# A job's float32 products with v issued as one operation, and the clamp of the weights moved from VectorE to GpSimd

## The chip, the cores and the metric

The kernel runs on one core of a Trainium2 chip. The time is that of one execution on the device, in microseconds (us). One core has five engines that work at their own pace and meet at semaphores: TensorE (PE in the profile, its weight loads PEld), VectorE (DVE), ScalarE (ACT), GpSimd (POOL), and SyncE (SP), which here only issues transfers. Each engine takes its instructions strictly in program order.

## The reference

Causal attention with a decay, over 8 batches of 8 heads (576 positions of 64 elements each), and behind it a layer of two matrices with a squared ReLU between them:

```
scores = q @ k.T / sqrt(64) + cum[:, None] - cum[None, :]     # cum = cumsum(log(clip(f)))
scores = where(above the diagonal, -1e9, scores)
attn = exp(scores - max) / (sum + 1e-9)
x = attn @ v                                                   # 4608 tokens x 512
out = maximum(x @ w_in, 0) ** 2 @ w_out                        # 512 -> 2048 -> 512
```

The two weight matrices come as 64-bit floats.

## The kernel before

**A table of operations.** The program is not written in the order in which it runs. It lists some 6,700 small operations, each with what it needs, which buffers it takes and gives back, a priority, and a cost from hand-written formulas (`pe`, `dve`, `act`, `pool`, `dma`). `Order.run` plays them through and emits each operation for the engine on which it can start soonest; this order is then fixed, and every engine runs its part of it one instruction after the other. So a changed cost, need or buffer moves instructions on all engines.

**Attention** is cut into 72 jobs. Jobs 0 to 7 (LOW) hold the first 256 positions of two heads of batches 0 and 1, jobs 8 to 23 (HIGH) the other 320 positions of one such head, the rest (FULL) a whole head. A job has units, one for each tile of 128 keys: 4 in a LOW job, 5 in a HIGH one, 6 in a FULL one. For a job, `mm` and `top` (lines 712 and 720) find each row's maximum on TensorE and VectorE, a small transfer (`col`, line 729) puts the maxima into a row of the operands, and then for each unit there is a score of two products (764, 768), the exponential on ScalarE (774), the mask on the diagonal tile on GpSimd (777), and the product with v, `av`. Jobs 0 to 27 are "whole": their exponentials stay in float32, and `av` is a single matrix product in TensorE's float32 mode (line 849), which takes four passes over the columns. The jobs behind them split the exponentials and v into two parts each and make three fast products of them (852 to 854). The results are copied to `xt` (873), and the sums (879, 882) go through two trips to memory (926, 934, 941) to be inverted and spread, after which `divide` (954) finishes a pair of heads.

**The layer** works on chunks of 256 tokens: 18 chunks, each with 16 steps of a first product (`m1`, line 1045), ReLU and square, and a second product (`m2`, 1074). Chunk 0 needs jobs 0 to 3, chunk 1 jobs 4 to 7; these two run side by side.

**The weights**, 32 tiles of 128 by 512, are turned from 64-bit words to a pair of fast-mode halves while chunk 0 runs: a transfer issued by GpSimd (432), the magnitude on ScalarE (435), then on VectorE the clamp of the exponent (439), `rebias` (443), `top` (450), `bottom` (456), a copy (316), and `lower` (464). Step `f` of chunk 0 cannot start before tiles `2f` and `2f + 1` are done.

**Buffers.** The exponentials of a whole job go in turn to the buffers named `ph` and `pl`, of which there are three each; a buffer is free again when its `av` is done. Two more, named `p`, serve the other jobs.

Of the kernel before, what the change touches and what calls it, by code (L numbers as in the profile page):

```python
# [9 lines left out]
F32 = mybir.dt.float32  # L10
# [4 lines left out]
ALU = mybir.AluOpType  # L15
# [79 lines left out]
class Order:  # L95
# [17 lines left out]
    def add(self, key, ways, emit, after=(), take=(), give=(), prio=0.0, slack=0.0):  # L113
        op = Op()
        op.key, op.ways, op.emit, op.prio, op.slack = key, ways, emit, prio, slack
        op.take, op.give = list(take), list(give)
        for b in op.give:
            b.users += 1
        op.then, op.ready, op.left = [], 0.0, 0
        op.number = len(self.ops)  # L120
        self.ops.append(op)
        assert key not in self.keys, key
        self.keys[key] = op
        op.left = list(after)
# [65 lines left out]
def pe(*columns, four=False):  # L190
    t = sum(1.68 * n + 10 if four else max(n / 2.2 + 3, 55) for n in columns)
    return "PE", t, t + 165, None


def dve(n, sources=1, psum=False):
    if psum:
        return "DVE", 70 + 1.04 * n, 160 + 1.04 * n, None
    per = 0.54 if sources == 1 else 1.045
    return "DVE", 65 + per * n, 150 + per * n, n >= 64
# [10 lines left out]
def pool(n, sources=1):  # L210
    return ("POOL", 200 + 2.1 * n, 250 + 2.1 * n, True) if sources == 2 else ("POOL", 60 + 1.85 * n, 60 + 1.85 * n, None)
# [8 lines left out]
def decay_attention_relu2_kernel(  # L220
# [18 lines left out]
    nc = tc.nc  # L239

    NH, D, _, S = qk.shape
    P = 2 * D
# [3 lines left out]
    NT, DM = out.shape  # L246
# [10 lines left out]
    MAG_LOW, MAG_HIGH = struct.unpack("<2f", struct.pack("<2I", 0x38000000, 0x47EFFFFF))  # L257
# [5 lines left out]
    DUAL = True  # L263
    BE = 2
    NLOW = BE * NPAIR
    DIRECT = 2
    SLACK_G, SLACK_C = 1500, 600

# [19 lines left out]
    add = order.add  # L288
# [5 lines left out]
    def named(name, shape, dtype):  # L294
        return lambda i: wk.tile(shape, dtype, name=f"{name}{i}", bufs=1)
# [4 lines left out]
    def bank(use):  # L300
# [7 lines left out]
            x=2, r=1, g=1, gh=2, gl=2, osb=2,  # L308
# [3 lines left out]
    def buf(kind, make=None):  # L312
        return Buffer(pools[kind], make)
# [102 lines left out]
    def weight(i):  # L416

        temp = buf("osb", named("osb", [P, DM], F32))
# [17 lines left out]

        def clamp(e):

            nc.vector.tensor_scalar(temp.tile, temp.tile, MAG_LOW, MAG_HIGH, ALU.max, ALU.min)

        def rebias(e):
            wi = temp.tile.bitcast(I32)
# [25 lines left out]
        w = lambda x, j=i: ("w", j, x)  # L468
# [6 lines left out]
        elif i >= 24:  # L475
            after += [("score", g, len(jobs[g]["units"]) - 1) for g in range(SETS)]
        p = weight_prio(i)
        add(w("stage"), [dma(8 * P * DM, "POOL", 2)], stage, after, prio=p)
        add(w("mag"), [act(DM)], magnitude, [w("stage")], take=[temp], prio=p)
        add(w("clamp"), [dve(DM)], clamp, [w("mag")], prio=p)  # L480
        add(w("rebias"), [dve(DM)], rebias, [w("clamp")], prio=p)
        add(w("top"), [dve(DM, 2)], top, [w("rebias")], prio=p)
        add(w("bottom"), [dve(DM, 2)], bottom, [w("top")], prio=p)
# [9 lines left out]
    LOW, HIGH, FULL = range(3)  # L493
    jobs = [
        dict(
            kind=LOW, heads=(2 * g, 2 * g + 1),
# [5 lines left out]
            kind=HIGH, heads=(h,),  # L502
# [5 lines left out]
            kind=FULL, heads=(h,),  # L508
# [26 lines left out]
    def job(g):  # L535
        st = jobs[g]
        kind, whole, units = st["kind"], st["whole"], st["units"]
        heads, h = st["heads"], st["heads"][0]
        b = h // H
        p = job_prio(g)  # L540
# [92 lines left out]
        give = [raw]  # L633
# [119 lines left out]
        for u, (i, j, q0, q1) in enumerate(units):  # L753
# [1 line left out]
            n, o = q1 - q0, i * QA  # L755
            ps = bank("s")
            if whole:
                pt = buf(("ph", "pl")[u % 2], named(("ph", "pl")[u % 2], [P, 448], F32))
            else:
                pt = buf("p", named("p", [P, 448], F32))  # L760

# [66 lines left out]
            jobs[g - 1]["den"] if g % 2 else buf("den", named("den", [P, S], F32))  # L828
        )
        done_copies = []  # L830
        for u, low in parts:
            i, j, q0, q1 = units[u]
            kn = KT[j][1]
            group = groups[i, low]
# [18 lines left out]
                nc.tensor.matmul(a[:D, oo], vvl, ph.tile[:, ii], start=False, stop=False)  # L853
                nc.tensor.matmul(a[:D + 1, oo], vvh, ph.tile[:, ii], start=False, stop=final)  # L854

            key = ("av", g, u) if low or kind == HIGH or u < NU - 2 else ("avh", g, u)
            n = s1_ - s0
            take = [acc] if first and (kind != LOW or i == 0) else []
            give = [x for x in (ph, pl) if x]
# [1 line left out]
            need = need + [last_av] + ([("v", g)] if whole else [("vl", g)])  # L861
            if whole and kind != LOW:
                need.append(("ones", g))
            add(key, [pe(n, four=True) if whole else pe(n, n, n)], av, need, take=take, give=give, prio=p - 0.4)
            last_av = key
            if final:
                def copy_x(e, acc=acc, i=i, low=low):
                    m = QA if low else S - QA
# [302 lines left out]
```

## Time and profile before

| | |
|---|---|
| median of 3 runs | 1214.35 us (1210.73 to 1215.1) |
| the profiled execution's own time | 1216.67 us |
| its span, from the first to the last instruction | 1214.9 us |
| TensorE busy | 1168.1 us, 96% of the span |
| VectorE, ScalarE, GpSimd busy | 684.7, 819.1, 392.5 us |
| mean granted clock of TensorE | 0.990 of full speed |

The profile's times are those of one profiled execution. An engine's busy time counts its own instructions; a busy TensorE is not TensorE at its peak, since the ends of its products are modelled and a product that waits inside counts as busy. The granted clock is the share of 2.4 GHz that TensorE was given: 1.00, or 0.50, which is 1.2 GHz.

### The profile page before, as it was taken

What the parts mean: (1) busy time and instruction counts of PE and PEld (TensorE: products, weight loads), DVE (VectorE), ACT (ScalarE), POOL (GpSimd) and SP (SyncE); (2) the same over time, 40 slices, a digit from 0 to 9 for tenths busy, and PEclk for the clock granted to TensorE, in tenths of its full rate; (3) what the DMA queues carried; (4) which work ended last, traced back from release to release, by engine and by line L of the source; (5) the groups of instructions that cost most, each with busy time, mean ns of one, the idle gap of its engine ahead of it and who ended that gap; (6) DMA issues with size and microseconds to landing.
All of it is one profiled execution on the core that took longest, in us unless ns stands there. A gap on an engine that the chain in (4) does not pass through costs nothing.

```text
span 1214.9 us, 23061 instructions
## 1 busy us (share of the span) xinstructions
PE 1168.1 (96%) x7572; PEld 1038.6 (85%) x7572; DVE 684.7 (56%) x1897; ACT 819.1 (67%) x2129; POOL 392.5 (32%) x593
## 2 busy tenths in 40 slices
PE   3779999999999999999999999999999999999998
PEld 2567777788998999999999999999999999999997
DVE  6779888973666656666667664256565642121111
ACT  3578776775876878787787776577767774454443
POOL 4524443412443444444344444034433420000000
PEclk9979999999999999999999999999999999999999
DMA  4455555421211212122212212021221110000000
GB/s 102 126 119 135 127 136 136 109 72 42 58 43 42 60 42 60 42 60 57 60 42 44 58 42 60 18 42 43 59 42 44 42 34 12 18 19 1 19 18 19
DMA packets 118869, 69.86 MB, mean 57 GB/s; under 512 B 98172, under 2 KB 102300, under 8 KB 118748
## 3 DMA queue, kind: packets, MB, share of 16 engines
q10 hardware_dynamic: 49408, 30.42, 10.5%
q1 hardware_dynamic: 63868, 20.12, 7.6%
q0 software_dynamic: 5472, 17.83, 5.1%
q8 instruction: 61, 1.00, 0.4%
q14 instruction: 60, 0.49, 0.1%
HBM read 58.14 MB, written 9.88 MB: 56 GB/s over the span
## 4 chain that ended last, share of the span: by engine, by line
PE 86%; DVE 5%; DMA 4%; issue 2%; ACT 1%; POOL 1%; SPq 0%; ACTq 0%; DVEq 0%; POOLq 0%
PE bank L1045 32%; PE bank L1074 31%; PE bank L764 4%; PE bank L712 4%; PE bank L768 4%; PE bank L849 3%; PE bank L854 3%; PE bank L853 3%; PE bank L852 3%; DMA w<-tcol 1%; DMA den<-rdr 1%; DVE bank L720 1%; DMA rdr<-cmp 1%; DMA up<-tcol 1%; DMA qkraw<-in_qk 1%
## 5 line engine op out<-in xcount | busy, mean ns | idle before, releaser
L1074 PE MATMUL bank<-w,gh 128*128 128x512 f32 x1152 | 411.8, 398 | 0.5 <-DVE w L464 0.4
L1045 PE MATMUL bank<-xh,w 128*128 128x256 f32 x2304 | 325.8, 284 | 2.7 <-ACT r L1051 1.0
L1045 PEld LDWEIGHTS bank<-xh,w 128*128 128x128 f32 x2304 | 303.8, 190 | 13.8 <-ACT r L1051 1.4
L1063 DVE TENSOR_TENSOR gl<-g,gh 128x256 fp32r<-128x256 f32 x288 | 143.6, 498 | 261.2 <-ACT gh L1060 187.0
L1074 PEld LDWEIGHTS bank<-w,gh 128*128 128x128 f32 x1152 | 216.9, 188 | 40.8 <-DVE w L464 1.0
L1074 PE MATMUL bank<-w,gl 128*128 128x512 f32 x576 | 227.3, 395 | 0.4 <-DVE gl L1063 0.4
L1051 ACT ACTIVATE r<-bank 128x256 f32<-128x256 f32 x288 | 110.3, 383 | 141.0 <-PE bank L1045 130.8
L720 DVE CUSTOM_DVE_ANT_0 bank<-bank,mz 128x448 f32<-128x448 f32 (+4 forms) x320 | 137.9, 432 | 113.9 <-PE bank L712 110.5
L777 POOL TENSOR_SCALAR_AFFINE_SELECT p<-p 128x128 f32<-128x128 f32 (+1 forms) x220 | 77.3, 353 | 332.0 <-ACT p L774 329.4
L1045 PE MATMUL bank<-xl,w 128*128 128x256 f32 x1152 | 183.6, 281 | 0.1
L1045 PEld LDWEIGHTS bank<-xl,w 128*128 128x128 f32 x1152 | 157.3, 190 | 0.3 <-DVE xl L1008 0.3
L805 DVE TENSOR_TENSOR pl<-p,ph 128x320 fp32r<-128x320 f32 (+3 forms) x220 | 134.5, 615 | 38.7 <-ACT ph L802 37.4
L1060 ACT ACTIVATE gh<-r 128x256 fp32r<-128x256 f32 x288 | 119.9, 416 | 46.4 <-PE bank L1074 38.3
L621 POOL TENSOR_TENSOR st<-qkraw,up 64x576 fp32r<-64x576 f32 x88 | 132.4, 1504 | 28.2 <-DVE up L316 13.6
L764 PE MATMUL bank<-up 67*128 67x192 f32 (+3 forms) x364 | 122.9, 338 | 5.0 <-DMA up<-tcol 3.0
L712 PE MATMUL bank<-up 66*128 66x448 f32 (+1 forms) x352 | 113.7, 330 | 14.2 <-DMA up<-w 14.0
L802 ACT CAST ph<-p 128x320 fp32r<-128x320 f32 (+3 forms) x220 | 98.0, 447 | 43.4 <-PE bank L854 16.8
L774 ACT ACTIVATE p<-bank 128x320 f32<-128x320 f32 (+4 forms) x264 | 101.5, 389 | 37.4 <-DVE pl L805 17.5
L1074 PEld LDWEIGHTS bank<-w,gl 128*128 128x128 f32 x576 | 108.8, 189 | 14.6 <-DVE gl L1063 1.1
L1055 ACT ACTIVATE g<-r 128x256 f32<-128x256 f32 x259 | 106.1, 410 | 3.4 <-DVE gl L1063 0.7
L768 PE MATMUL bank<-st 128*128 128x192 f32 (+3 forms) x364 | 108.0, 298 | 0.0
L712 PEld LDWEIGHTS bank<-up 66*128 66x128 f32 x352 | 65.5, 189 | 18.7 <-issue 14.3
(103 smaller groups left out, 1635.3 us busy)
## 6 DMA issues: line engine op xcount, KB each, us to landing
qkraw<-in_qk ACTq DMA_DIRECT2D x48, 288.0 KB
v<-in_v ACTq DMA_DIRECT2D x64, 160.0 KB
out<-osb SPq DMA_DIRECT2D x35, 256.0 KB
w<-in_w_in POOLq DMA_DIRECT2D x32, 256.0 KB, 3.7
w<-in_w_out POOLq DMA_DIRECT2D x32, 256.0 KB, 4.6
den<-rdr SPq DMA_DIRECT2D x48, 144.0 KB
up<-tcol SPq DMA_DIRECT2D x232, 0.5 KB
qkraw<-in_qk ACTq DMA_DIRECT2D x11, 224.0 KB
```

Source lines behind the costliest of these rows:

```text
L621: (nc.vector if e == "DVE" else nc.gpsimd).tensor_tensor(out=out, in0=in0, in1=in1.bitcast(F32), op=ALU.subtract,)
L712: nc.tensor.matmul(ps.tile[:m, :n], r2[:D + 2, o + q0:o + q0 + m], kl0[:D + 2, o + k0:o + k0 + n], start=True, stop=True,)
L720: nc.vector.tensor_tensor_reduce(out=ps.tile[:m, :n], in0=ps.tile[:m, :n], in1=mz[:m, mo:mo + n], op0=ALU.add, op1=ALU.min, scale=-1.0, sc ...
L764: nc.tensor.matmul(ps.tile[:kn, :n], kl0[:D + 3, o + k0:o + k0 + kn], r2[:D + 3, o + q0:o + q1], start=True, stop=False,)
L768: nc.tensor.matmul(ps.tile[:kn, :n], l2[:, o + k0:o + k0 + kn], r1[:, o + q0:o + q1], start=False, stop=True,)
L805: nc.vector.tensor_tensor(out=pl.tile[:kn, :n], in0=pt.tile[:kn, :n], in1=ph.tile[:kn, :n].bitcast(F32), op=ALU.subtract,)
L1045: nc.tensor.matmul(ph.tile[:, :T], w[:, s, cc], x[:, cc, :], start=(cc == 0 and k == 0), stop=(cc == NCC - 1 and k == 2),)
L1051: nc.scalar.activation(out=r.tile, in_=ph.tile[:, :T], func=AF.Relu)
L1055: nc.scalar.activation(out=g.tile, in_=r.tile, func=AF.Square)
L1060: nc.scalar.activation(out=gh.tile, in_=r.tile, func=AF.Square)
L1063: nc.vector.tensor_tensor(out=gl.tile, in0=g.tile, in1=gh.tile.bitcast(F32), op=ALU.subtract)
L1074: nc.tensor.matmul(po, x[:, ts], w[:, s], start=(fc == 0 and k == 0), stop=(fc == NF - 1 and k == 2),)
```

## The change

In a whole job the products with v are collected and issued as one operation, back to back: the four of a LOW job, the five of a HIGH job, and in a FULL job the first four and then the last three. Such an operation needs the exponentials and masks of all its units, and gives all their buffers back together. A table `WHERE` says to which kind of buffer each unit's exponential goes; the third unit now goes to one of the two `p`. The clamp of the weights is issued to GpSimd, with the cost `pool(512)` in the table.

```
@@ -263,6 +263,8 @@
     DUAL = True
     BE = 2
     NLOW = BE * NPAIR
+    WHERE = ("ph", "pl", "p", "ph", "pl", "ph", "pl")
+    TOGETHER = [4, 5, 4]
     DIRECT = 2
     SLACK_G, SLACK_C = 1500, 600
 
@@ -436,7 +438,7 @@
 
         def clamp(e):
 
-            nc.vector.tensor_scalar(temp.tile, temp.tile, MAG_LOW, MAG_HIGH, ALU.max, ALU.min)
+            nc.gpsimd.tensor_scalar(temp.tile, temp.tile, MAG_LOW, MAG_HIGH, ALU.max, ALU.min)
 
         def rebias(e):
             wi = temp.tile.bitcast(I32)
@@ -477,7 +479,7 @@
         p = weight_prio(i)
         add(w("stage"), [dma(8 * P * DM, "POOL", 2)], stage, after, prio=p)
         add(w("mag"), [act(DM)], magnitude, [w("stage")], take=[temp], prio=p)
-        add(w("clamp"), [dve(DM)], clamp, [w("mag")], prio=p)
+        add(w("clamp"), [pool(DM)], clamp, [w("mag")], prio=p)
         add(w("rebias"), [dve(DM)], rebias, [w("clamp")], prio=p)
         add(w("top"), [dve(DM, 2)], top, [w("rebias")], prio=p)
         add(w("bottom"), [dve(DM, 2)], bottom, [w("top")], prio=p)
@@ -755,7 +757,8 @@
             n, o = q1 - q0, i * QA
             ps = bank("s")
             if whole:
-                pt = buf(("ph", "pl")[u % 2], named(("ph", "pl")[u % 2], [P, 448], F32))
+                x = WHERE[u]
+                pt = buf(x, named(x, [P, 448], F32))
             else:
                 pt = buf("p", named("p", [P, 448], F32))
 
@@ -828,7 +831,10 @@
             jobs[g - 1]["den"] if g % 2 else buf("den", named("den", [P, S], F32))
         )
         done_copies = []
-        for u, low in parts:
+
+        size = TOGETHER[kind] if whole else 1
+        together = []
+        for x, (u, low) in enumerate(parts):
             i, j, q0, q1 = units[u]
             kn = KT[j][1]
             group = groups[i, low]
@@ -853,7 +859,8 @@
                 nc.tensor.matmul(a[:D, oo], vvl, ph.tile[:, ii], start=False, stop=False)
                 nc.tensor.matmul(a[:D + 1, oo], vvh, ph.tile[:, ii], start=False, stop=final)
 
-            key = ("av", g, u) if low or kind == HIGH or u < NU - 2 else ("avh", g, u)
+            end = parts[min(x - x % size + size, len(parts)) - 1]
+            key = ("av", g, *end)
             n = s1_ - s0
             take = [acc] if first and (kind != LOW or i == 0) else []
             give = [x for x in (ph, pl) if x]
@@ -861,8 +868,23 @@
             need = need + [last_av] + ([("v", g)] if whole else [("vl", g)])
             if whole and kind != LOW:
                 need.append(("ones", g))
-            add(key, [pe(n, four=True) if whole else pe(n, n, n)], av, need, take=take, give=give, prio=p - 0.4)
-            last_av = key
+            if whole:
+                together.append((av, n, need, take, give))
+                if (u, low) == end:
+                    avs, ns, needs, takes, gives = zip(*together)
+                    together = []
+
+                    def all_av(e, avs=avs):
+                        for f in avs:
+                            f(e)
+
+                    add(
+                        key, [pe(*ns, four=True)], all_av, sum(needs, []), take=sum(takes, []), give=sum(gives, []), prio=p - 0.4,
+                    )
+                    last_av = key
+            else:
+                add(key, [pe(n, n, n)], av, need, take=take, give=give, prio=p - 0.4)
+                last_av = key
             if final:
                 def copy_x(e, acc=acc, i=i, low=low):
                     m = QA if low else S - QA
```

Three places of the order show what moved. On TensorE, at the first jobs (L849 before and L855 now are products with v, L764/L767 and L768/L771 the two products of a score, L712/L714 products for the maxima; `bank_244` before and `bank_271` now are the result of job 0), before:

```order
L849 MATMUL bank_244<-ph_228,w_83 65x256
L764 MATMUL bank_248<-up_71 128x128
L768 MATMUL bank_248<-st_77 128x128
L712 MATMUL bank_251<-w_74,w_73 128x256
L849 MATMUL bank_244<-pl_237,w_83 65x128
L712 MATMUL bank_259<-w_74,w_73 128x128
L849 MATMUL bank_244<-ph_246,w_83 65x256
L764 MATMUL bank_271<-up_72 128x256
L768 MATMUL bank_271<-st_78 128x256
```

and now:

```order
L767 MATMUL bank_246<-up_71 128x128
L771 MATMUL bank_246<-st_77 128x128
L714 MATMUL bank_249<-w_74,w_73 128x256
L714 MATMUL bank_256<-w_74,w_73 128x128
L767 MATMUL bank_264<-up_72 128x256
L771 MATMUL bank_264<-st_78 128x256
L714 MATMUL bank_268<-w_74,w_73 128x256
L855 MATMUL bank_271<-ph_228,w_83 65x256
L855 MATMUL bank_271<-pl_237,w_83 65x128
L855 MATMUL bank_271<-p_244,w_83 65x256
L855 MATMUL bank_271<-ph_252,w_83 65x128
```

The four products stand together behind the job's last score and the first scores and maxima of the next jobs, where they used to stand each behind its own mask.

On GpSimd, at the masks of jobs 2 to 4 (L777/L780), before:

```order
L777 AFFINE_SELECT ph_344<-ph_344 128x128
L777 AFFINE_SELECT pl_347<-pl_347 128x128
L777 AFFINE_SELECT ph_373<-ph_373 128x128
L777 AFFINE_SELECT pl_378<-pl_378 128x128
L777 AFFINE_SELECT ph_411<-ph_411 128x128
L777 AFFINE_SELECT pl_427<-pl_427 128x128
L777 AFFINE_SELECT ph_443<-ph_443 128x128
L777 AFFINE_SELECT pl_455<-pl_455 128x128
```

and now, with the first two clamps (L441) and a transfer of a weight tile (L434):

```order
L780 AFFINE_SELECT ph_336<-ph_336 128x128
L780 AFFINE_SELECT pl_352<-pl_352 128x128
L780 AFFINE_SELECT p_381<-p_381 128x128
L780 AFFINE_SELECT ph_384<-ph_384 128x128
L441 TENSOR_SCALAR osb_408<-osb_408 128x512
L780 AFFINE_SELECT ph_436<-ph_436 128x128
L780 AFFINE_SELECT pl_439<-pl_439 128x128
L780 AFFINE_SELECT p_443<-p_443 128x128
L780 AFFINE_SELECT ph_463<-ph_463 128x128
L434 DMA w_479<-in_w_in 128x2x256 x2
L441 TENSOR_SCALAR osb_475<-osb_475 128x512
```

A clamp stands ahead of the four masks of job 3, and another ahead of those of job 4.

On SyncE's queue, at jobs 6 and 7 (`w_73<-tcol` and `w_75<-tcol` are the maxima of jobs 6 and 7, L729/L731, four of each; `den<-rdr` is the spread of the inverted sums of jobs 2 and 3, L941/L963), before:

```order
L729 DMA w_73<-tcol_574 1x128x1 x2
L941 DMA den_420<-rdr_107 64x2x256 x2
L729 DMA w_73<-tcol_574 1x128x1 x2
L729 DMA w_75<-tcol_618 1x128x1 x2
L926 DMA cmp_642<-den_562 128x1x8
L577 DMA up_71<-cum_dr 2x576
L729 DMA w_75<-tcol_618 1x128x1 x2
```

and now:

```order
L731 DMA w_73<-tcol_533 1x128x1 x4
L956 DMA rdr_107<-cmp_526 128x8
L731 DMA w_75<-tcol_601 1x128x1
L579 DMA up_71<-cum_dr 2x576
L731 DMA w_75<-tcol_601 1x128x1 x2
L963 DMA den_429<-rdr_107 64x2x256 x2
L731 DMA w_75<-tcol_601 1x128x1
```

The spread stood between the maxima of job 6 and now stands ahead of the last of job 7.

## Rows read from the trace of the kernel before

**Rows 1.** The page: busy time by engine; the granted clock in 40 slices.
```profile
PE 1168.1 (96%) x7572; PEld 1038.6 (85%) x7572; DVE 684.7 (56%) x1897; ACT 819.1 (67%) x2129; POOL 392.5 (32%) x593
...
PEclk9979999999999999999999999999999999999999
```

**Rows 2.** Stretches in us: length, busy time by engine, granted clock, DMA share, GB/s.
```profile
18.00:74.00 56.00, 38.12 (x142) 30.10 (x143) 35.69 (x110) 28.39 (x72) 22.79 (x46) 0.85 0.47 113
74.00:100.00 26.00, 23.37 (x133) 18.66 (x132) 22.14 (x63) 22.66 (x57) 10.79 (x20) 0.93 0.51 131
100.00:130.00 30.00, 30.00 (x183) 25.28 (x182) 27.80 (x69) 23.32 (x58) 13.07 (x23) 1.00 0.45 119
130.00:270.00 140.00, 133.69 (x769) 106.90 (x769) 116.27 (x297) 98.96 (x247) 52.46 (x96) 0.99 0.49 121
270.00:320.00 50.00, 50.00 (x324) 43.91 (x325) 22.06 (x72) 32.02 (x80) 13.53 (x24) 1.00 0.17 36
320.00:1215.00 895.00, 889.83 (x6018) 810.93 (x6017) 446.65 (x1254) 606.80 (x1607) 272.07 (x365) 1.00 0.17 40
```

**Rows 3.** Waits of PE from 17 to 100 us: total, times, longest.
```profile
PE bank L764 <- DMA w<-tcol: 6.3, 3, 3.8
PE bank L849 <- POOL ph L777: 5.8, 4, 3.2
PE bank L764 <- DMA up<-tcol: 3.0, 2, 1.9
```

**Rows 4.** Timeline of PE at 228 us: start, length, instruction.
```profile
228.61 0.39 PE L1074 MATMUL bank<-w,gl 128*128 128x512 f32 x1
228.85 0.40 PE L1074 MATMUL bank<-w,gh 128*128 128x512 f32 x1
229.17 0.33 PE L849 MATMUL bank<-pl,v 64*65 64x64 f32 x2
...
229.68 0.31 PE L768 MATMUL bank<-st 128*128 128x320 f32 x1
229.84 0.70 PE L849 MATMUL bank<-ph,v 128*65 128x320 f32 x2
...
230.52 0.32 PE L768 MATMUL bank<-st 128*128 128x320 f32 x1
230.67 0.52 PE L1045 MATMUL bank<-xh,w 128*128 128x256 f32 x3
```

**Rows 5.** Line 439, the clamp: ns shortest/median/longest, first and last start.
```profile
L439 DVE TENSOR_SCALAR osb<-osb x32: 408/420/516, 46.3 to 245.0; 128x512 f32<-128x512 f32 x32
```

**Rows 6.** Lines 777 and 621 on POOL, in the same form.
```profile
L777 POOL TENSOR_SCALAR_AFFINE_SELECT pl<-pl x60: 228/312/1334, 19.8 to 306.2; 128x128 f32<-128x128 f32 x40, 64x64 f32<-64x64 f32 x20
L777 POOL TENSOR_SCALAR_AFFINE_SELECT ph<-ph x40: 282/299/2002, 19.6 to 302.2; 128x128 f32<-128x128 f32 x40
...
L621 POOL TENSOR_TENSOR st<-qkraw,up x88: 1410/1430/2016, 290.0 to 972.0; 64x576 fp32r<-64x576 f32 x88
```

**Rows 7.** Groups on POOL, 60 to 150 us: count, busy us, mean ns, idle before.
```profile
L777 POOL TENSOR_SCALAR_AFFINE_SELECT ph<-ph 128x128 f32<-128x128 f32 x12 | 6.8, 569 | 13.4 <-ACT ph L774 13.4
L777 POOL TENSOR_SCALAR_AFFINE_SELECT pl<-pl 128x128 f32<-128x128 f32 x12 | 5.3, 442 | 32.3 <-ACT pl L774 32.3
```

**Rows 8.** Timelines of POOL and of DVE at 90 us.
```profile
90.50 2.00 POOL L777 TENSOR_SCALAR_AFFINE_SELECT ph<-ph 128x128 f32<-128x128 f32 x1
...
90.47 0.68 DVE L450 SCALAR_TENSOR_TENSOR osb<-w,osb 128x512 int32<-128x512 int32 x1
91.07 0.68 DVE L464 TENSOR_TENSOR w<-osb,w 128x512 fp32r<-128x512 f32 x1
91.67 0.68 DVE L456 SCALAR_TENSOR_TENSOR osb<-w,osb 128x512 int32<-128x512 int32 x1
```

**Rows 9.** Timeline of PE at 193 us, with idle time before it; chain of waits there.
```profile
193.37 1.18 PE L849 MATMUL bank<-pl,v 128*65 128x320 f32 x2 [1.35 <-POOL pl L777]
...
186.34 5.26 DMA den<-rdr
```

More of the change, by code (lines that the diff above doesn't have):

```diff
@@ L265, in decay_attention_relu2_kernel @@
     NLOW = BE * NPAIR
+    WHERE = ("ph", "pl", "p", "ph", "pl", "ph", "pl")
+    TOGETHER = [4, 5, 4]
     DIRECT = 2
@@ L437, in clamp @@
         def clamp(e):
-            nc.vector.tensor_scalar(temp.tile, temp.tile, MAG_LOW, MAG_HIGH, ALU.max, ALU.min)
+            nc.gpsimd.tensor_scalar(temp.tile, temp.tile, MAG_LOW, MAG_HIGH, ALU.max, ALU.min)
         def rebias(e):
@@ L479, in weight @@
         add(w("mag"), [act(DM)], magnitude, [w("stage")], take=[temp], prio=p)
-        add(w("clamp"), [dve(DM)], clamp, [w("mag")], prio=p)
+        add(w("clamp"), [pool(DM)], clamp, [w("mag")], prio=p)
         add(w("rebias"), [dve(DM)], rebias, [w("clamp")], prio=p)
@@ L757, in job @@
             if whole:
-                pt = buf(("ph", "pl")[u % 2], named(("ph", "pl")[u % 2], [P, 448], F32))
+                x = WHERE[u]
+                pt = buf(x, named(x, [P, 448], F32))
             else:
@@ L830, in job @@
         done_copies = []
-        for u, low in parts:
+        size = TOGETHER[kind] if whole else 1
+        together = []
+        for x, (u, low) in enumerate(parts):
             i, j, q0, q1 = units[u]
@@ L854, in av @@
                 nc.tensor.matmul(a[:D + 1, oo], vvh, ph.tile[:, ii], start=False, stop=final)
-            key = ("av", g, u) if low or kind == HIGH or u < NU - 2 else ("avh", g, u)
+            end = parts[min(x - x % size + size, len(parts)) - 1]
+            key = ("av", g, *end)
             n = s1_ - s0
@@ L863, in job, with all_av @@
                 need.append(("ones", g))
-            add(key, [pe(n, four=True) if whole else pe(n, n, n)], av, need, take=take, give=give, prio=p - 0.4)
-            last_av = key
+            if whole:
+                together.append((av, n, need, take, give))
+                if (u, low) == end:
+                    avs, ns, needs, takes, gives = zip(*together)
+                    together = []
+                    def all_av(e, avs=avs):
+                        for f in avs:
+                            f(e)
+                    add(
+                        key, [pe(*ns, four=True)], all_av, sum(needs, []), take=sum(takes, []), give=sum(gives, []), prio=p - 0.4,
+                    )
+                    last_av = key
+            else:
+                add(key, [pe(n, n, n)], av, need, take=take, give=give, prio=p - 0.4)
+                last_av = key
             if final:
```

## The prediction

> **What bounds the kernel now.** I read the page first. TensorE is busy 96% of the span, no other engine over 67% [rows 1], so the end moves only where TensorE gets less to do or stands idle less. The table of stretches says where it is idle: 17.9 us of 56 before 74 us, 2.6 of the next 26, nothing from 100 to 130, 6.3 of 140 to 270, nothing to 320, and behind that 5.2 of 895 [rows 2]. All whole jobs and all clamps lie before 320 us, so what the change can give or take has to come out of these 26.8 us of idle time (17.9 + 2.6 + 6.3), or be added to them. VectorE is the fullest of the others just there: 27.8 of 30 us and 116.3 of 140 [rows 2]. The clock matters as well: the row of the page gives 7 tenths in the third slice, and the first stretch has 0.85 on average [rows 1, 2], so TensorE spends part of the LOW jobs at 1.2 GHz. Its waits there are for transfers of the maxima (6.3 and 3.0 us) and for masks from GpSimd (5.8 us) [rows 3].
>
> **The products as one operation.** The number of products, 140 (8 x 4 + 16 x 5 + 4 x 7), and their columns stay. What could be saved is a cost of going from the fast mode to float32 and back. The timeline shows none for products with 128 keys: from the start of one with 320 columns at 229.84 to the next kind of work at 230.67 are 0.83 us, of which the score between them takes two products of about 0.15 (230.52 to 230.67 for one), and the 0.53 left are four passes of 320 columns at 2.4 GHz, 4 x 320 / 2400 = 0.53 [rows 4]. The product with 64 keys does cost more: from 229.17 to 229.84 less the same 0.30 are 0.37 us, where its four passes of 64 columns take 0.11, and the step to it is 0.32 instead of 0.24 [rows 4]. That makes 0.34 us too much in each of the 20 HIGH and FULL whole jobs, 6.8 us in all. In the new order this product still stands between products with 128 keys, so whatever is paid to enter and leave the 64 rows should stay: I take 0, with 6.8 us gained as the other bound.
>
> What the grouping adds is delay. In a LOW job the first three products used to run while later masks were still to come; now all four follow the last mask, three of them later than before. Three quarters of 4 x 768 columns are 2304, 1.9 us at 1.2 GHz. That delays the job's result, and with it chunk 0, only where the results of jobs 2 and 3 end last. They need not: the transfer that held TensorE longest there is that of the maxima, up to 3.8 us [rows 3], which stood behind the spread of the inverted sums in SyncE's queue. In the new queue the spread stands ahead of the last maximum of job 7, and not between those of job 6, so the wait moves one job on and does not go. I take 0 for the LOW jobs, between 5 us lost (the burst of 1.9 us and one further wait like the mean of the masks' and the maxima's longest, 3.2 to 3.8) and 5 us gained (the 6.3 us of waits for maxima all but gone).
>
> **The clamp leaves VectorE.** 32 clamps at a median of 0.42 us, between 46 and 245 us [rows 5], are 13.4 us less for VectorE, 7% of its time there. TensorE stands idle 8.9 us between 74 and 270 us (2.6 + 6.3) [rows 2]. No gain can pass that; below, nothing is gained if none of it hangs on VectorE. Much of it shows as waits for transfers and for ScalarE and GpSimd, with VectorE somewhere ahead of them, so I take a third, 3.0 us.
>
> **The clamp arrives on GpSimd.** The trace has no such operation there. One source and one result over 64 and 128 columns take 0.23 and 0.29 us at best (the mask), so 512 columns at that slope, about 1 ns a column, make 0.29 + 384 x 0.001 = 0.7 us; two sources over 576 columns take 1.43 us [rows 6], and by columns 512 / 576 x 1.43 = 1.27. I take 1.0, between them, as it has one source and four times the columns. But GpSimd is not alone: from 60 to 150 us the masks of 128 columns take 0.50 us on average ((6.8 + 5.3) / 24) [rows 7] instead of 0.29, and one took 2.00 us while VectorE ran three instructions with two tensors each, back to back from 90.47 to 92.35 [rows 8]. So a clamp is 1.0 x 0.50 / 0.29 = 1.7 us in this stretch, and 32 of them 55 us, on an engine that is busy 52.5 of 140 us and 13.1 of 30 [rows 2]. It has the room. The cost is order: behind a clamp in GpSimd's queue stand masks, behind a mask stands the product, and now a whole job's products. Such a wait is seen at 193 us: a division at the head of the queue waited for a transfer (5.26 us on the chain), the mask behind it was late, TensorE stood 1.35 us [rows 9]. The clamp's own head-of-queue wait is for the magnitude on ScalarE; and `rebias` on VectorE now waits for GpSimd, with maxima queued behind it. I charge 1.5 us: one clamp in eight (4) shows as a wait of 0.4. Bounds: nothing, if all masks keep their slack; 11 us, if one in three shows as 1 us.
>
> The Trainium skill (GPSIMD Engine Reference, Key points) says that GpSimd shares its SBUF interfaces with VectorE and contends with VectorE's instructions that use two ports or two SBUF inputs. The mask of 2.00 us agrees; taken alone the rule speaks against this change, and its result is the second rival below.
>
> **The sum.** 0 for the products, 0 for the LOW jobs, -3.0 for VectorE, +1.5 for GpSimd: -1.5 us. The profiled execution took 1216.67 us, 1.8 more than its span and 2.3 more than the median of 1214.35; from the median this gives 1212.8, said as 1213. A measurement of this kernel can tell about 0.5% from no change, 6.1 us: faster is below 1208.3, slower above 1220.4.
>
> **The rivals.**
> *VectorE was the brake after all.* It is over 90% busy from 100 to 130 us and 83% from there to 270 [rows 2]. If all 8.9 us of idle time behind 74 us go, and some 2 to 5 of the LOW jobs' waits, the time is 1214.35 - 11 to - 14, about 1202. For it: the idle time ends where VectorE's load ends, at 270 us. Against: TensorE is never idle from 100 to 130 us, where VectorE is fullest.
> *GpSimd becomes the brake.* Clamps in front of masks, drawn out by VectorE's two-tensor instructions; if one in three costs TensorE 1 us, 11 us come on top of no gain: 1225. It decides from a clamp of about 2.5 us, or when magnitudes come late. For it: the mask of 2.00 us. Against: GpSimd idles over half of this time, and its wait of 5.26 us at 193 us cost TensorE only 1.35.
> *The LOW jobs get later.* The three products behind the last mask and one more wait: +5 to +8 against -1.5, 1219 to 1221. For it: 17.9 us of idle time show that nothing is spare there. Against: at 1.2 GHz TensorE has other maxima and scores to do meanwhile.
> *The two parts do nothing that counts.* 1214, within my forecast's own spread.
>
> **How the numbers follow.** My forecast with the last case, 1208 to 1219: 0.50. First rival 0.27, second 0.15, third 0.08, half of it on either side of the bound. Faster 0.27 and 0.02 from the forecast's edge: 0.29. Slower 0.15 + 0.04: 0.19. Same: 0.52. Below 1203 lies a little over a third of the first rival, 0.10, and above 1223 two thirds of the second, 0.10: the range is 1203 to 1223.
>
> **What would show it.** The 128-key products should still take 0.53 us for 320 columns within a group, and the 64-key one 0.34 too much; if the latter is gone, that step was wrong and up to 6.8 us are gained. VectorE's busy time should fall by about 13 us; GpSimd's clamps should take 1.0 us alone and 1.7 on average. TensorE's idle time from 74 to 270 us should go from 8.9 to about 7, with more of it put down to masks. The first `m1` should start at about the same time. I am wrong if the LOW jobs end several us earlier or later (their clock may change with the bursts), or if the work behind 320 us, which I left alone, takes another time than now.

## The result, and the profile after

The changed kernel took 1218.95 us (median of 11 runs, 1213.09 to 1222.26) where the kernel before took 1215.01 (11 runs, 1210.73 to 1218.66): a ratio of 1.0036, 95% interval 1.002 to 1.0052. It is slower by 0.36%, 3.9 us, where 1.5 us less was forecast.

The page of the changed kernel, busy time by engine, granted clock, and the chain that ended last, by engine:

```profile
PE 1167.0 (96%) x7572; PEld 1033.7 (85%) x7572; DVE 685.5 (56%) x1872; ACT 805.7 (66%) x2122; POOL 447.1 (37%) x625
...
PEclk9689999899999999999999999999999999999999
...
PE 81%; POOL 4%; DVE 4%; DMA 4%; issue 3%; ACT 2%; SPq 0%; ACTq 0%; DVEq 0%; POOLq 0%
```

GpSimd is 54.6 us busier than in [rows 1], which looks like the forecast's 55 us of clamps, but is not: the 32 clamps take 64.9 us, and the masks 9.5 less than before (112.8 against 122.3). VectorE gave up 13.7 us of clamps and is as busy as before over the whole span (685.5 against 684.7). On the chain that ended last GpSimd has 4%.

The same stretches as in [rows 2], of the changed kernel (length, busy time of TensorE, its weight loads, VectorE, ScalarE and GpSimd, granted clock, DMA share, GB/s; the last one ends with its span):

```profile
18.00:74.00 56.00, 38.26 (x162) 29.30 (x163) 35.32 (x112) 34.10 (x84) 31.25 (x54) 0.73 0.47 117
74.00:100.00 26.00, 21.84 (x129) 16.76 (x128) 21.62 (x55) 19.59 (x51) 14.88 (x23) 0.99 0.52 129
100.00:130.00 30.00, 29.37 (x169) 23.39 (x170) 26.73 (x63) 23.02 (x57) 22.74 (x26) 1.00 0.58 141
130.00:270.00 140.00, 130.91 (x750) 105.25 (x749) 112.49 (x267) 89.45 (x232) 86.36 (x108) 0.96 0.41 111
270.00:320.00 50.00, 50.00 (x315) 42.39 (x314) 20.92 (x66) 30.12 (x77) 14.04 (x25) 1.00 0.18 40
320.00:1220.50 900.50, 893.55 (x6045) 813.90 (x6043) 454.28 (x1278) 602.46 (x1613) 269.97 (x370) 1.00 0.16 40
```

TensorE's idle time from 74 to 270 us is 4.16 + 0.63 + 9.09 = 13.9 us instead of 8.9, and its clock from 130 to 270 is 0.96 instead of 0.99. Before 74 us the idle time is the same (17.7 against 17.9), but the first `m1` starts at 72.8 us instead of 74.1. So 1.3 us are won ahead of it and 5.0 lost behind it, 3.7 in all, near the 3.9 between the medians. (The two profiled executions lie 5.6 us apart, 1222.26 and 1216.67.)

The clock of the first stretch, 0.73 here and 0.85 in [rows 2], can't be read off that column: it counts all time ahead of the trace's first record of the clock as 1.00. In the kernel before that record, a rise, comes at 53.6 us. Ahead of it products of 256 columns start 0.21 to 0.22 us after each other, which is 256 / 1200, where from 80 us on they start 0.12 us after each other:

```profile
34.41 0.41 PE L764 MATMUL bank<-w,w 67*128 67x256 f32 x1
34.63 0.41 PE L768 MATMUL bank<-w,w 128*128 128x256 f32 x1
34.84 0.31 PE L712 MATMUL bank<-w,w 66*128 66x128 f32 x1
```

So from 18 to 74 us the kernel before had 2.4 GHz for 3.4 us only (a mean of 0.53), and the changed kernel, whose first record is a rise at 23.5 us, had it for 20.5 us (0.68). The clock of the LOW jobs went up with the change, not down.

Waits of TensorE in the changed kernel, 17 to 100 us (total, times, longest), which answer to [rows 3]:

```profile
PE bank L855 <- POOL ph L780: 6.0, 1, 6.0
PE bank L855 <- POOL pl L780: 3.8, 1, 3.8
PE bank L767 <- issue: 3.5, 1, 3.5
```

and from 100 to 330 us:

```profile
PE bank L1096 <- DVE w L466: 5.8, 6, 2.2
PE bank L714 <- DVE tcol L722: 2.8, 4, 1.3
```

In the LOW jobs the waits for the maxima's transfers have gone from the head of the list, and two long ones for the group's last mask stand there. They belong to the group and not to the clamp: they end at 30.9 and 35.8 us, ahead of the first clamp at 41.6. Behind 100 us no mask is waited for: what TensorE waits for is `lower` of a weight tile (`L466`), the last step of the way on which the clamp stands. The clamp's own row (ns shortest/median/longest, first and last start) and who waited for it:

```profile
L441 POOL TENSOR_SCALAR osb<-osb x32: 1907/1933/2853, 41.6 to 241.5; 128x512 f32<-128x512 f32 x32
...
who waited for it (us, times):
  DVE osb L445: 12.2, 13
```

The shortest of 32 took 1.91 us and the median 1.93. One clamp beside which VectorE ran nothing at all (at 221.8 us) took 1.93. So it is the price of the instruction alone, where the forecast had 1.0. `rebias` on VectorE waited 12.2 us for it. One such place on the chain of waits (start, length, what), and the end of it on TensorE's timeline:

```profile
184.68 2.37 POOL osb L441
...
188.03 0.72 POOL w L434
...
189.27 3.07 DMA den<-rdr
...
192.48 1.18 POOL xt L976
193.66 1.89 POOL osb L441
195.55 0.75 POOL w L434
...
197.46 2.37 POOL osb L441
...
199.85 0.45 DVE osb L445
...
204.12 0.61 DVE w L466
```

```profile
204.78 0.80 PE L1096 MATMUL bank<-w,gh 128*128 128x512 f32 x1 [2.22 <-DVE w L466]
```

From 184 to 200 us the chain runs through GpSimd: three clamps, the transfers of the next weight tiles that it issues (`L434`, 0.72 and 0.75 us), and a division (`L976`) that stood at the head of its queue for a transfer of 3.07 us with a clamp behind it. The tile is late, TensorE stands 2.22 us. Its clock is at 1.2 GHz from 204.4 to 207.8 us and, around the next such place, from 228.3 to 235.2; before, it fell once in this stretch, for 3.4 us.

### The profile page after: what moved, and what is told of

It is laid out like the page before. It is cut to its first block, busy times and chain, and to the rows that moved or that the text cites. A ratio compares the mean times of both kernels' runs of the same rounds, so it can differ in the third digit from the quotient of the medians.

```text
span 1220.5 us, 22937 instructions
## 1 busy us (share of the span) xinstructions
PE 1167.0 (96%) x7572; PEld 1033.7 (85%) x7572; DVE 685.5 (56%) x1872; ACT 805.7 (66%) x2122; POOL 447.1 (37%) x625
## 4 chain that ended last, share of the span: by engine, by line
PE 81%; POOL 4%; DVE 4%; DMA 4%; issue 3%; ACT 2%; SPq 0%; ACTq 0%; DVEq 0%; POOLq 0%
PE bank L1096 31%; PE bank L1067 30%; PE bank L767 3%; PE bank L714 3%; PE bank L771 3%; PE bank L860 3%; PE bank L859 3%; PE bank L858 2%; PE bank L855 2%; DMA den<-rdr 2%; POOL osb L441 2%; DMA rdr<-cmp 1%; POOL w L434 1%; DVE bank L722 1%; DVE st L623 0%
## 5 line engine op out<-in xcount | busy, mean ns | idle before, releaser
L1085 DVE TENSOR_TENSOR gl<-g,gh 128x256 fp32r<-128x256 f32 x288 | 147.4, 512 | 263.7 <-ACT g L1077 220.7
L780 POOL TENSOR_SCALAR_AFFINE_SELECT p<-p 128x128 f32<-128x128 f32 (+1 forms) x248 | 84.4, 342 | 340.9 <-ACT p L777 337.3
L777 ACT ACTIVATE p<-bank 128x320 f32<-128x320 f32 (+4 forms) x292 | 110.8, 383 | 38.8 <-DVE pl L808 15.9
L714 PE MATMUL bank<-up 66*128 66x448 f32 (+1 forms) x352 | 110.1, 321 | 18.4 <-DMA up<-w 10.6
L767 PE MATMUL bank<-up 67*128 67x192 f32 (+3 forms) x364 | 113.1, 312 | 2.1 <-DMA up<-tcol 1.9
L771 PE MATMUL bank<-st 128*128 128x192 f32 (+3 forms) x364 | 107.5, 297 | 0.0
L714 PEld LDWEIGHTS bank<-up 66*128 66x128 f32 x352 | 64.6, 187 | 23.0 <-issue 14.5
```

The costliest lines, as they stand in the source:

```text
L714: nc.tensor.matmul(ps.tile[:m, :n], r2[:D + 2, o + q0:o + q0 + m], kl0[:D + 2, o + k0:o + k0 + n], start=True, stop=True,)
L767: nc.tensor.matmul(ps.tile[:kn, :n], kl0[:D + 3, o + k0:o + k0 + kn], r2[:D + 3, o + q0:o + q1], start=True, stop=False,)
L771: nc.tensor.matmul(ps.tile[:kn, :n], l2[:, o + k0:o + k0 + kn], r1[:, o + q0:o + q1], start=False, stop=True,)
L777: nc.scalar.activation(out=pt.tile[:kn, :n], in_=ps.tile[:kn, :n], func=AF.Exp, scale=SCALE)
L1085: nc.vector.tensor_tensor(out=gl.tile, in0=g.tile, in1=gh.tile.bitcast(F32), op=ALU.subtract)
```

## The experiments

All ratios are to the kernel before, run on the same chip; intervals are 95%. The kernel before had medians of 1214.15 to 1215.30 us on these chips, so medians of different experiments can be set against each other to about 1 us.

**1. The group without the move: the clamp back on VectorE.**

```
-            nc.gpsimd.tensor_scalar(temp.tile, temp.tile, MAG_LOW, MAG_HIGH, ALU.max, ALU.min)
+            nc.vector.tensor_scalar(temp.tile, temp.tile, MAG_LOW, MAG_HIGH, ALU.max, ALU.min)
...
-        add(w("clamp"), [pool(DM)], clamp, [w("mag")], prio=p)
+        add(w("clamp"), [dve(DM)], clamp, [w("mag")], prio=p)
```

> The grouped products alone, with the clamp back on VectorE. In the profile of the changed kernel a clamp on GpSimd takes 1.93 us instead of the 1.0 that I took and that the order's table counts, and TensorE waits for finished weights. If the slow clamp is what costs (theory A), this kernel stands at the time before or up to 4 us under it, 1211 to 1215. If the grouping costs (theory B: bursts behind the last mask, buffers given back together, VectorE's relief not enough), it stands 4 us or more above the time before, 1219 or more.

1206.13 us, ratio 0.9926 (0.9904 to 0.9948). Grouping alone gains 0.74%, 8.9 us. Its first `m1` starts at 68.1 us, and from 74 to 270 us TensorE is idle for 5.0 us:

```profile
74.00:270.00 196.00, 191.04 (x1132) 154.69 (x1131) 168.09 (x430) 145.11 (x369) 73.19 (x133) 0.99 0.47 119
```

6.0 us ahead of `m1` and 3.9 behind it (8.9 less 5.0) make 9.9, near the 8.9 between the medians.

**2. The move without the group**, the same two edits the other way in the kernel before.

> The clamp on GpSimd alone, each product with v issued by itself as before. Theory A: about 4 us above the time before, 1219. Theory B: at the time before or under it, since VectorE loses 13 us of work, 1211 to 1215.

1236.66 us, ratio 1.0182 (1.0156 to 1.0207). With the table's price of 1007 ns the move costs 21.6 us by itself, more than the 12.8 that it costs in the grouped kernel (1218.95 less 1206.13), so the two parts of the change don't simply add up: from 74 to 270 us TensorE is idle for 20.1 us, and VectorE waits 15.8 us for the clamps.

**3 and 4. The clamp's true price in the table**, in the changed kernel and in the one of the second experiment. The instruction is the same; only the order moves.

```
-        add(w("clamp"), [pool(DM)], clamp, [w("mag")], prio=p)
+        add(w("clamp"), [("POOL", 1950, 1950, None)], clamp, [w("mag")], prio=p)
```

> The changed kernel with one number of the table changed: the clamp on GpSimd is counted as 1950 ns instead of 1007, so that the order is made for the duration that the trace shows. Theory A in the form that the wrong price is the harm: 3 to 5 us less than the changed kernel, so about the time before, and fewer waits of VectorE's rebias for the clamp (12.2 us in the changed kernel). Theory A in the form that the duration itself is the harm, or theory B: within 1.5 us of the changed kernel.

> The kernel before with the clamp on GpSimd at its true price of 1950 ns. If the wrong price is the harm, at the time before or up to 3 us under it; if the duration, like the kernel with the clamp alone at the lower price, about 4 us above the time before; if the grouping, at the time before.

With the group 1214.54 us, 0.9999 (0.9982 to 1.0016); without it 1216.29, 1.0004 (0.9988 to 1.0019). So an order made for 1007 ns costs 4.4 us with the group and 20.4 without it. VectorE's wait for the clamps falls from 12.2 to 4.3 us in the grouped kernel, and from 15.8 to nothing in the other. With the right price the grouped kernel's first `m1` starts at 68.6 us and not at 72.8: these 4.2 us are nearly all that the wrong price cost. What is left against the first experiment is 8.4 us, and it lies behind `m1`, where TensorE is still idle for 12.8 us instead of 5.0:

```profile
74.00:270.00 196.00, 183.24 (x1049) 145.54 (x1048) 167.43 (x405) 135.49 (x344) 130.22 (x162) 0.97 0.48 118
```

Without the group it is otherwise. There the move with the right price costs nothing that can be told (1.0004), although GpSimd is as busy in this stretch, and TensorE is idle for 9.8 us, where it was 8.9:

```profile
74.00:270.00 196.00, 186.20 (x1073) 150.19 (x1072) 169.34 (x408) 142.57 (x359) 134.61 (x167) 0.98 0.49 122
```

So the 8.4 us are no fixed price of moving the clamps: they are lost in the grouped kernel alone. Whether the group makes GpSimd's time dearer, or the table happened to find the better order without it, is not shown.

**5, 6 and 7. The group in parts**, all with the clamp on VectorE and the new buffers: no group, LOW alone, HIGH and FULL alone.

```
-    TOGETHER = [4, 5, 4]
+    TOGETHER = [1, 1, 1]
...
+    TOGETHER = [4, 1, 1]
...
+    TOGETHER = [1, 5, 4]
```

> The new table of buffers alone (the third unit's exponential in one of the two p), every product its own operation, the clamp on VectorE. Grouping with the clamp on VectorE gave 0.9926 of the time before. If the two further buffers are the gain (theory C), this keeps most of it: 1206 to 1209. If the grouping is (theory D: bursts of four passes that hold TensorE's clock up, and fewer places where a late mask stops the queue), this stands at 1212 to 1217.

> Only the LOW jobs' four products as one operation, HIGH and FULL ones singly, new buffers, clamp on VectorE. Of the gain of the grouping about 7 us of work are already won at 100 us of the trace, where mostly LOW jobs ran. If the LOW jobs carry it, 1206 to 1209; if the HIGH and FULL ones do, near the kernel with the new buffers alone.

> The complement: LOW products singly, those of the HIGH and FULL jobs grouped, new buffers, clamp on VectorE. If the LOW jobs carry the gain, 1211 to 1216; if the others do, 1206 to 1209.

No group: 1221.53 us, 1.0056 (1.0039 to 1.0072), so the third buffer alone makes it slower by 0.56%, some 7 us. LOW alone: 1214.14, 0.9996 (0.998 to 1.0013), 7.4 less than without a group. HIGH and FULL alone: 1211.08, 0.9974 (0.9963 to 0.9985), 10.4 less. The two gains are different: LOW alone brings the first `m1` from 74.5 to 65.7 us, and the idle time from 74 to 270 us stays at some 11 to 12 us; HIGH and FULL leave `m1` at 74.1 us and bring that idle time from 12.3 to 7.2.

**8. Either engine**: the clamp goes to the engine on which the table can start it soonest, GpSimd at 1950 ns.

```
-        add(w("clamp"), [pool(DM)], clamp, [w("mag")], prio=p)
+        add(w("clamp"), [dve(DM), ("POOL", 1950, 1950, None)], clamp, [w("mag")], prio=p)
```

> Grouped products, and the order may put each clamp on VectorE or on GpSimd (at its true price of 1950 ns), whichever is done sooner; 10 of 32 go to GpSimd. All on VectorE took 1206.1 us, all on GpSimd at the true price 1214.5. If a clamp on GpSimd harms only where it comes at a bad time, this is at 1206 or a little under it; if each one harms by its length, about a third of the 8.4 us between the two, 1209.

10 of the 32 clamps go to GpSimd; 1209.13 us, 0.9952 (0.9936 to 0.9969). It lies between VectorE alone (1206.13) and GpSimd alone (1214.54), at about a third of the way with about a third of the clamps.

**9. GpSimd's time beside the weights.** The first experiment, and for each weight tile two operations on GpSimd on a tile of its own that nothing needs (added work).

```
+                nc.gpsimd.tensor_scalar(decoy, decoy, MAG_LOW, MAG_HIGH, ALU.max, ALU.min)
...
+        add(w("aside"), [("POOL", 1950, 1950, None)], aside, [w("mag")], prio=p)
```

> Grouped products and clamps on VectorE, which took 1206.1 us; in addition GpSimd does, for each weight tile, two operations of the clamp's kind over 256 columns on a scratch tile that nobody reads, at the clamp's true price of 1950 ns. The weights do not wait for it. If it is GpSimd's time that the moved clamp costs (masks and transfers queued behind it), this is as slow as all clamps on GpSimd at the true price, about 1214. If it is the longer way of the weights (ScalarE, GpSimd, VectorE), it stays at 1206 to 1208.

1223.05 us, 1.006 (1.0034 to 1.0087). But the two took 2.48 us together, not 1.95, so this one mixed occupancy with a wrong price; the last experiment mends that.

**10. The price by itself**, one run of the changed kernel with other forms of the clamp: every fourth without the minimum (so this part of the clamp is left out there), every fourth in two halves.

```
+            if i % 4 == 1:
+                nc.gpsimd.tensor_scalar(temp.tile, temp.tile, MAG_LOW, None, ALU.max)
+            elif i % 4 == 2:
+                for x in (temp.tile[:, :DM // 2], temp.tile[:, DM // 2:]):
+                    nc.gpsimd.tensor_scalar(x, x, MAG_LOW, MAG_HIGH, ALU.max, ALU.min)
```

> The changed kernel, where every fourth clamp on GpSimd does the maximum alone and leaves the minimum out, and another fourth is done in two halves of 256 columns. It shows the price only. If the two operations on each element make the 1.93 us, the single one takes 1.0 to 1.3; if the columns do, a half takes about 1.0; if the start does, a half takes well over 1.2.

The rows of the three forms (whole, without the minimum, halves):

```profile
L447 POOL TENSOR_SCALAR osb<-osb x16: 1908/1920/2388, 41.1 to 239.6; 128x512 f32<-128x512 f32 x16
...
L442 POOL TENSOR_SCALAR osb<-osb x8: 1487/1574/2427, 45.7 to 229.1; 128x512 f32<-128x512 f32 x8
...
L445 POOL TENSOR_SCALAR osb<-osb x16: 1052/1062/1593, 52.7 to 235.5; 128x256 f32<-128x256 f32 x16
```

256 columns more cost 1908 - 1052 = 856 ns, 3.3 ns a column, and 1052 - 856 = 0.2 us is the start. The forecast had 1 ns a column, from the mask. The second operation is 0.42 us of the 1.91.

**11 and 13. The clock in the LOW jobs.** Both add work to the kernel without a group (experiment 5) and leave its order alone. The first issues the first product of each LOW score four times; the second puts two products of 256 columns in the float32 mode ahead of each LOW score of 256 positions.

```
+                    m = 4 if kind == LOW else 1
+                    for x in range(m):
...
+                if kind == LOW and n == 256:
+                    for _ in range(2):
+                        nc.tensor.matmul(ps.tile[:P, :256], fill[:, :P], fill, start=True, stop=True)
```

> The kernel with the new buffers and single products (1221.5 us, whose TensorE ran at 1.2 GHz until 73 us), the same order and table, but the first product of each LOW score issued four times, the last one counting: 18,432 columns more, 7.7 us of TensorE at 2.4 GHz and 15.4 at 1.2. If bursts raise the clock and the clock is what grouping the LOW jobs gains (theory D), stretches at 2.4 GHz appear before 73 us, and the time stays within 3 us of 1221.5 or falls in spite of the added work. If the order of the queue is the gain, the clock may rise but the time goes up by 4 us or more.

> This is the kernel with the new buffers, single products and the clamp on VectorE (1221.53 us, first m1 at 74.5 us), in an unchanged order, to which two float32 products of 256 columns are added ahead of each score of 256 positions in the LOW jobs: 16 x 2 x 4 x 256 = 32,768 more columns, 13.7 us at 2.4 GHz and 27 at 1.2. Theory A, the clock is what the group gains in the LOW jobs: such bursts bring 2.4 GHz in well before 73 us, and the first m1 comes at 74 to 80 us in spite of the added work, with 2.4 GHz shown in several stretches from 30 us on. Theory B, the group gains by the order and not by the clock: bursts don't change the clock before 70 us, and the first m1 comes some 15 us or more later, 88 to 95 us.

The first took 1232.27 us, 1.0143 (1.0118 to 1.0167): TensorE was busy 50.4 of the 56 us from 18 to 74, and yet the trace has the clock rise first at 83.2 us (73.3 in experiment 5, without the added work). It says nothing on the gain, since the clock was not brought up earlier. The second took 1220.74 us, 1.0043 (1.0027 to 1.006), against 1221.53 without the added work. Its stretches (clock in the third column from the end):

```profile
34.00:41.00 7.00, 3.64 (x24) 2.84 (x24) 5.85 (x16) 3.51 (x9) 4.07 (x7) 0.96 0.79 206
41.00:44.20 3.20, 3.20 (x11) 2.54 (x12) 0.00 (x0) 0.67 (x2) 0.00 (x0) 0.54 0.32 83
44.20:67.50 23.30, 16.35 (x96) 12.87 (x94) 19.05 (x63) 16.05 (x39) 8.50 (x19) 1.00 0.50 109
67.50:71.00 3.50, 3.01 (x10) 2.58 (x11) 3.44 (x8) 1.92 (x5) 1.25 (x2) 0.54 0.28 67
```

and its products with v from 34 to 66 us beside those of the kernels without added work (busy us, mean ns), first experiment 5, then this one, then experiment 1:

```profile
L855 PE MATMUL bank<-ph,w 128*65 128x256 f32 x8 | 4.4, 653 | 4.0 <-POOL ph L780 3.9
```

```profile
L860 PE MATMUL bank<-ph,w 128*65 128x256 f32 x8 | 2.5, 392 | 2.9 <-POOL ph L785 2.8
```

```profile
L855 PE MATMUL bank<-ph,w 128*65 128x256 f32 x12 | 4.5, 467 | 0.7 <-POOL ph L780 0.7
```

With the added bursts the clock is at 2.4 GHz for most of 34 to 67 us. The work that was there before took 38.0 us of TensorE from 18 to 74; with the added products, whose records cover 19.3 us, it is 41.4 for all of it. The first `m1` starts at 74.8 us, 0.2 later than without 32,768 columns of added work. So these bursts in the float32 mode raise the clock, in an unchanged order. They differ from the added products of experiment 11 in more than the mode (128 rows where those have 67, and all ones as data), and which of these counts is not shown. The grouped products are bursts in the float32 mode too: in experiment 1 the trace has 2.4 GHz for 20.5 us before the first `m1`, in the kernel before for 3.4. The time at 2.4 GHz doesn't fix when `m1` starts: the changed kernel also has 20.5 us of it and starts at 72.8, and experiment 2, with 3.4 us, starts at 71.0.

**12. The group with the old buffers**, third unit back to `ph` (and the clamp on VectorE).

```
-    WHERE = ("ph", "pl", "p", "ph", "pl", "ph", "pl")
+    WHERE = ("ph", "pl", "ph", "pl", "ph", "pl", "ph")
```

> Grouped products with the clamp on VectorE, and the exponentials in ph and pl in turn as before, without p. The new buffers alone made the kernel 0.56% slower than before. If the new table of buffers is a burden in itself, this is at 1200 to 1204; if a group needs the two further buffers so that the next job's exponentials can start, it is above 1208.

1205.78 us, 0.9933 (0.9911 to 0.9954): the same as experiment 1. The third kind of buffer is not what the group gains by, and in a group it doesn't cost either.

**14. GpSimd's time beside the weights, rightly priced**: experiment 9 with 2480 ns in the table.

```
-        add(w("aside"), [("POOL", 1950, 1950, None)], aside, [w("mag")], prio=p)
+        add(w("aside"), [("POOL", 2480, 2480, None)], aside, [w("mag")], prio=p)
```

> The group with the clamp on VectorE (1206.13 us), and beside each weight tile two products on GpSimd on a tile of its own, which nothing needs, now planned at 2480 ns, what they took (the run before planned them at 1950 and took 1223.05). Theory A, GpSimd's time itself is what costs the 8 us that are left when the clamp is priced rightly: with more time taken than the clamps took (79 us against 62), about 1214 or above. Theory B, the longer way of a weight tile costs them: nothing waits for this work, the order knows its length, and the time stays at 1206 to 1209.

1214.63 us, 1.0011 (0.9993 to 1.0028): 8.5 us above experiment 1, though nothing needs the added work and the table has about its length (2.48 us; it took 2.58 on average). Its stretch from 74 to 270 us, and TensorE's longest waits in it:

```profile
74.00:270.00 196.00, 176.98 (x1011) 141.08 (x1012) 168.40 (x409) 135.02 (x341) 144.14 (x183) 0.97 0.46 116
```

```profile
PE bank L862 <- POOL ph L787: 4.9, 3, 4.5
PE bank L774 <- ACT pl L784: 2.8, 1, 2.8
PE bank L1074 <- DVE w L472: 2.8, 2, 2.0
```

TensorE is idle for 19.0 us there (the profiled execution, with a span of 1218.5 us, is one of the longer of this kernel), and its longest wait is for a mask. So taking GpSimd's time is enough to lose such an amount in the grouped kernel. How it is lost is left open: masks and transfers stand behind the added work in GpSimd's queue, but VectorE's instructions get longer beside it as well (`rebias` takes 486 ns on average in this stretch, 429 in experiment 1). The added work is longer than the clamps (82.5 us of GpSimd against 64.9), so a part of the 8.4 us may still be the weights' longer way; these runs don't split it.

## Why the prediction was wrong

The time lies in the range, on the other side of no change than forecast. Two terms were mis-sized by several us: -8.9 us for the group (0 forecast) and, on top of it, +12.8 for the clamp (-3.0 + 1.5 forecast). They have opposite signs and largely cancel, and it is by this luck that the time is within 6 us of 1213. The split depends on which part goes first: taken first, the clamp costs 21.6 us (experiment 2), and the group then gains 17.7 (1236.66 less 1218.95).

**The failed step: the charge for the clamp on GpSimd, 1.5 us, and the price under it.** "I take 1.0, between them, as it has one source and four times the columns." It took 1.91 at its shortest, outside both ends (0.7 and 1.27). The row that was scaled, the mask at 1 ns a column, is another operation; the clamp costs 3.3 ns a column (experiment 10). But GpSimd's time was nearly right: the factor for contention made 1.7 us and 55 in all of the 1.0, and 2.03 and 64.9 were measured. That was luck, a price too low times a factor that doesn't apply to the clamp's median. What went wrong by far more is what this time costs TensorE, "one clamp in eight (4) shows as a wait of 0.4", and its upper bound of 11 us. In its place: the move costs 12.8 us in the grouped kernel (1218.95 less 1206.13). Of these, 4.4 go to an order made with 1007 ns (experiment 3), a term that the prediction does not have; 8.4 remain with the true price, and such an amount can be lost there by taking GpSimd's time alone (experiment 14). That the charge isn't the same everywhere shows without the group, where the move at the true price costs nothing that can be told (experiment 4). Why the grouped kernel pays and the other doesn't stays open.

The second rival, with its "clamp of about 2.5 us", had the engine and the sign right. What it named as the wait, masks behind clamps, is not what TensorE waits long for: its two long waits for masks end before the first clamp starts, and behind 100 us it waits for `lower`.

**The factor for contention** (0.50 / 0.29) is not in the clamp's median, 1.93 us against 1.91 at its shortest, but both engines pay something. On GpSimd 11 of the 32 clamps took 2.0 to 2.85 us. On VectorE the row of `rebias` from 74 to 270 us shows it, changed kernel and experiment 1 (busy us, mean ns, idle before):

```profile
L445 DVE TENSOR_SCALAR osb<-osb 128x512 int32<-128x512 int32 x29 | 15.3, 527 | 12.0 <-POOL osb L441 11.8
```

```profile
L441 DVE TENSOR_SCALAR osb<-osb 128x512 f32<-128x512 f32 x28 | 13.1, 469 | 1.0 <-ACT osb L437 0.9
...
L445 DVE TENSOR_SCALAR osb<-osb 128x512 int32<-128x512 int32 x29 | 12.3, 429 | 0.0
```

The Trainium skill (GPSIMD Engine Reference, Key points) names contention with VectorE's instructions in a two-port mode or with two SBUF inputs, without saying who pays. Here `rebias` takes 429 ns on average with the clamps on VectorE and 527 with them on GpSimd. In the changed kernel the seven beside which GpSimd ran nothing took 0.42 us, and the five beside a clamp 0.63 on average. The larger part of the rise is not the clamps' own: the three that ran beside a division (`L976`) and a mask behind it took 0.77 to 1.12 us. Nor is it always VectorE that pays: a `rebias` at 78.1 us took 0.42, and the clamp that started 0.11 us behind it took 2.08. The same page (Engine selection) calls GpSimd "roughly line-rate" for one input and sends elementwise maxima to VectorE. The measurement is against the first, 1.91 us against 0.42 [rows 5], and for the second.

**VectorE's relief, -3.0.** VectorE's busy time was to fall by 13 us; over the whole span it rose by 0.8. This sum mixes two things. Up to 320 us it fell by 6.9 (238.07 to 231.19), with 50 instructions fewer done by then; behind 320 us, where no clamp runs, it rose by 7.6 (446.65 to 454.28). Of the 13.7 us of clamps 2.9 came back as longer `rebias`, and VectorE now waits 12.2 us for the clamps. No relief shows in TensorE's time. The first rival falls with it: experiment 1, with the clamp still on VectorE, is at 1206, and with 10 and 32 clamps off VectorE it is 1209 and 1214.5 (experiments 8 and 3).

**The products, 0.** The part on the fast mode and the 64-key product was right. A group of the changed kernel on TensorE's timeline:

```profile
111.88 0.70 PE L855 MATMUL bank<-pl,v 128*65 128x320 f32 x2
112.41 0.49 PE L855 MATMUL bank<-p,v 128*65 128x192 f32 x2
112.83 0.33 PE L855 MATMUL bank<-ph,v 64*65 64x64 f32 x2
113.09 0.75 PE L855 MATMUL bank<-pl,v 128*65 128x320 f32 x2
```

From the product of 320 columns to the next are 0.53 us, as in [rows 4]. From the one of 192 columns to the end of the one with 64 keys are 0.68 (112.41 to 113.09), where their passes need 0.32 + 0.11; the extra of 0.25 us stays, in all 20 such jobs, a little less than the 0.34 before. But "I take 0" for the group was wrong: it gains 8.9 us against the kernel before.

**The LOW jobs, 0 between -5 and +5.** The forecast weighed what a later burst delays, at 1.2 GHz, and treated the clock as given. It read "part of the LOW jobs at 1.2 GHz" off the 0.85; it was all but 3.4 us of that stretch, so there was more to gain than it took. Float32 bursts can change the clock (experiment 13), and the first `m1` comes 6.0 us earlier in experiment 1. In the changed kernel it is 1.3, since the wrong price gives most of that back (5.5 earlier in experiment 3). That the clock makes the gain in the LOW jobs is not shown, only that such bursts raise it in an unchanged order.

**HIGH and FULL jobs.** That the group shortens idle time there (12.3 to 7.2 us, experiments 5 and 7) was not foreseen. Which wait goes isn't settled: without the group TensorE's waits in this stretch are many and small, the largest 1.6 us. Part of any such difference is the order that the table happens to give, as the buffers' 7 us in experiment 5 show, which vanish in a group (experiment 12).

## What to carry to other kernels

Price an operation on another engine by the same operation on it, or hold the bound as open as the nearest rows are far; a table of operations that decides the order needs that measured price too, since a price half the true one cost 4.4 us here with the group and 20.4 without. An engine that is half idle isn't always free when other work's transfers and masks stand in its queue: with the right price the same move cost 8.4 us in one kernel and nothing that can be told in the other, so an effect measured in one order is not a price. Where TensorE's granted clock is low in a stretch, ask of each edit whether it changes the clock and not only the work: the best version here, the group with the clamp left on VectorE (1206 us), beats both kernels, and 6 us of its gain lie in the stretch where the clock changed.

## What was not expected of the hardware

A two-operation maximum and minimum of 128x512 floats takes 1.91 us on GpSimd and 0.42 on VectorE. Beside such operations instructions of VectorE and of GpSimd both can get longer: `rebias` took 0.42 us alone and up to 1.12 beside a division on GpSimd, and the clamps 1.91 to 2.85. And a busy TensorE isn't one at 2.4 GHz: with added products in the fast mode it was busy 50.4 of 56 us and the trace has no 2.4 GHz before 83.2 us (experiment 11), while bursts in the float32 mode brought it for most of 34 to 67 us, with TensorE busy 41.4 of the 56 (experiment 13).
